# Attention scores contracted over 128 rows in four column strips instead of over 32 rows in 32x32 tiles

## The chip, the cores and the metric

The kernel runs on one core of a Trainium2 chip. The metric is the device time of one execution in microseconds (us), median over several executions. A profile is one such execution; its span runs from the first to the last instruction, so it is a little shorter than the metric. TensorE is called PE below, its weight loads PEld, VectorE DVE, ScalarE ACT, GpSimd POOL. "Granted clock" is the share of full speed that PE's clock was given. Each run has a state, fast or slow; only fast runs are compared. What is said here of the chip is read from the profiles and runs of this case, or called a reading or an estimate.

## The reference, cut to what matters

A block with a memory: 64 segments of 32 tokens, one after the other, each with 8 memory tokens that the segment before produced. 32 heads of 128 dimensions, then a feed-forward layer (FFN) with squared ReLU. Layer norms and residuals around both.

```python
for s in range(n_seg):                       # 64, a serial chain through mem
    h = jnp.concatenate([mem, xs], axis=1)   # 8 + 32 tokens, 640 wide
    q, k, v = (einsum('btd,dhe->bhte', h, W) for W in (Wq, Wk, Wv))   # 32 heads x 128
    scores = jnp.einsum('bhqe,bhke->bhqk', q, k) * scale
    p = _softmax(jnp.where(mask, scores, -1e9), axis=-1)
    o = jnp.einsum('bhte,hed->btd', jnp.einsum('bhqk,bhke->bhqe', p, v), Wo)
    mem = o[:, :M]
    outs.append(o[:, M:])
# h = x + attention; out = h + w2 . relu(w1 . norm(h) + b1)^2 + b2
```

## The kernel before

One block is four segments (`sp` = 0 to 3); a call of `step` handles one segment. The 40 keys of a segment are split: a main part of 32 (8 memory tokens and 24 of the segment's own) and a tail part with the last 8, which is kept for the four segments of a block together. The projections of q, k and v (`ps`) put four quarters of the output side by side on four strips of 32 partitions. ACT copies them to bf16 and DVE transposes them in 32x32 squares. In this kernel a strip `g` held whole heads, so after the transpose a head lay as four squares (`eb`) of 32 rows on one strip, and a score needed four matmuls that each contract over 32 rows:

```python
for g in range(G):                                   # masks: 16 matmuls
    r = slice(32 * g, 32 * g + 32)
    for c in range(G):
        nc.tensor.matmul(A(g)[32 * c:32 * c + 32, 0:AC], lhsT=id32[r, :], rhs=mask[r, sp, :], start=True, ...)
for lhsT, q1, off, n in ((kT, NQ, 0, NQ), (kt, 16, MC, 16)):   # main keys, then tail keys
    for i2 in range(2):
        for eb in range(4):
            for c in range(G):
                bl = (i2 * 4 + c) * 4 + eb
                for g in range(G):                   # 2 x 2 x 4 x 4 x 4 = 256 matmuls
                    r = slice(32 * g, 32 * g + 32)
                    nc.tensor.matmul(A(g)[32 * c:32 * c + 32, off + i2 * n:off + (i2 + 1) * n],
                                     lhsT=lhsT[r, bl, :], rhs=qT[r, bl, 0:q1], start=False, stop=(eb == 3), ...)
for t in range(2):
    nc.scalar.activation(out=p[:, 2 * t:2 * t + 2], in_=A2[t][:, :, 0:AC], func=ACT.Exp, scale=SCALE)
run(full, ...)       # a slice of FFN matmuls on PE while ACT computes Exp
# ... pz = sums over keys (2 matmuls), Ln, Exp, again a slice of FFN, pn = p * rz (2 DVE products)
# ... values: 64 matmuls of 32x128 tiles, main and tail keys alternating, then oT <- A
run(strip, ...)      # units of the next block's projections (pst) while oT is copied
wo_units(...)        # pw: 128 matmuls of 128x32 tiles, 160 columns each
run(strip, ...)      # more units while o goes to the next segment's HT
```

`full` and `strip` are lists of PE work of other blocks that fills the waits of the serial chain. `HT` is the input of a segment, transposed; a segment can't begin before the one before it has given its `o`.

The softmax here doesn't subtract the row's maximum and nothing guards it: scores larger than these inputs give would overflow.

Of the kernel before, what the change touches and what calls it, by code (L numbers as in the profile page):

```python
# [7 lines left out]
ACT = mybir.ActivationFunctionType  # L8
ALU = mybir.AluOpType
F32 = mybir.dt.float32  # L10
BF16 = mybir.dt.bfloat16
ET = mybir.EngineType

D, H, E, M, SEG, S, F = 640, 32, 128, 8, 32, 2048, 1728
G = 4
# [5 lines left out]
TL = 8  # L21
NQ = 40
# [3 lines left out]
SCALE = float(E) ** -0.5  # L26
EPS = 1e-5
NEG = -30000.0
MC = 2 * NQ
AC = MC + 32  # L30
PO = 128


@with_exitstack
def memory_transformer_kernel(ctx, tc, xa, xb, mem0, wq_d, wk_d, wv_d, wo_d, cst, wf_d, b1_d, out):
    nc = tc.nc
    pool = lambda name, bufs, **k: ctx.enter_context(tc.tile_pool(name=name, bufs=bufs, **k))
    const = pool("const", 1)
    s1, s2, s3, s4 = pool("s1", 1), pool("s2", 2), pool("s3", 3), pool("s4", 4)
    wfp = pool("wfp", WB)  # L40
    mm = pool("mm", 4, space=bass.MemoryType.PSUM)
    at = pool("at", 1, space=bass.MemoryType.PSUM)
# [4 lines left out]
    o_main = dram.tile([S // SEG, G, SEG, DG], BF16)  # L47
    o_tail = dram.tile([NB, G, SEG, DG], BF16)

    cs = const.tile([128, 128 + 128 + 32 + 4 * AC], BF16)  # L50
    ident, onesblk, id32 = cs[:, 0:128], cs[:, 128:256], cs[:, 256:288]
    mask = cs[:, 288:].rearrange("p (s a) -> p s a", s=4)
    wq, wk, wv = (const.tile([128, DC, H * E], BF16, name=n) for n in ("wq", "wk", "wv"))
    wo = const.tile([128, H, D], BF16)
    eps_t = const.tile([128, 1], F32)
# [33 lines left out]
    def flush():  # L89
        while late:  # L90
            late.pop(0)[1]()
# [14 lines left out]
    def run_side(n):  # L106
        while side and n > 0:
            side.pop(0)()
            n -= 1
# [71 lines left out]
    def blocks(row):  # L181
        return row[:].rearrange("p (b r) -> p b r", r=32)

    def half(w, lhs, n, vr=None):
        ps = mm.tile([128, 512], F32, tag="mm", name="ps")
        pass_units(w, lhs, n, ps)
        if vr is not None:
            nc.scalar.copy(out=vr[:, n * 512:(n + 1) * 512], in_=ps[:])  # L188
            return None
        row = s4.tile([128, 512], BF16, tag="row", name="row")  # L190
        nc.scalar.copy(out=row[:], in_=ps[:])  # L191
        return row
# [135 lines left out]
    def step(b, sp):  # L328
        HT, tl = HTs[b], tails[b]
        lhs = lambda c: HT[:, c * 128 + 32 * (3 - sp):c * 128 + 32 * (4 - sp)]  # L330
        qT = s1.tile([128, 32, NQ], BF16, tag="qT", name="qT")
        kT = s1.tile([128, 32, SEG], BF16, tag="kT", name="kT")
        vr = s1.tile([128, 1024], BF16, tag="vr", name="vr")
        qt = tl["q"][:].rearrange("p (b s t) -> p b s t", s=4, t=TL)
        nc.gpsimd.tensor_copy(out=qT[:, :, 0:TL], in_=qt[:, :, sp, :])
        for w, dst in ((wq, lambda n: qT[:, n * 16:(n + 1) * 16, TL:NQ]),
                       (wk, lambda n: kT[:, n * 16:(n + 1) * 16, :])):
            for n in range(2):
                row = half(w, lhs, n)
                nc.vector.transpose(out=dst(n), in_=blocks(row))  # L340
                run_side(1)
        for n in range(2):
            half(wv, lhs, n, vr)
            run_side(1)

        A2 = [at.tile([128, 2, 512], F32, tag=f"A{t}", name="A") for t in range(2)]

        def A(g):
            return A2[g // 2][:, g % 2]
        for g in range(G):  # L350
            r = slice(32 * g, 32 * g + 32)
            for c in range(G):
                nc.tensor.matmul(A(g)[32 * c:32 * c + 32, 0:AC], lhsT=id32[r, :], rhs=mask[r, sp, :], start=True,  # L353
                                 stop=False, skip_group_check=True)
        kt = tl["k"][:].rearrange("p (b r) -> p b r", r=32)
        for lhsT, q1, off, n in ((kT, NQ, 0, NQ), (kt, 16, MC, 16)):
            for i2 in range(2):
                for eb in range(4):
                    for c in range(G):
                        bl = (i2 * 4 + c) * 4 + eb  # L360
                        for g in range(G):
                            r = slice(32 * g, 32 * g + 32)
                            nc.tensor.matmul(A(g)[32 * c:32 * c + 32, off + i2 * n:off + (i2 + 1) * n],  # L363
                                             lhsT=lhsT[r, bl, :], rhs=qT[r, bl, 0:q1], start=False, stop=(eb == 3),
                                             skip_group_check=True)
        p = s1.tile([128, G, AC], BF16, tag="p", name="p")
        for t in range(2):
            nc.scalar.activation(out=p[:, 2 * t:2 * t + 2], in_=A2[t][:, :, 0:AC], func=ACT.Exp, scale=SCALE)  # L368
        share = sum(u[0] for u in full) / ((FS - sp) % 4 + 1)
        run(full, 0.84 if share > 1.9 else share / 2)  # L370
        flush()

        pz = mm.tile([128, 512], F32, tag="mm", name="pz")
        nc.tensor.matmul(pz[:, 0:320].rearrange("p (g a) -> p g a", g=G), lhsT=onesblk, rhs=p[:, :, 0:MC],  # L374
                         start=True, stop=False, skip_group_check=True)
        nc.tensor.matmul(pz[:, 0:320].rearrange("p (g i q) -> p g i q", g=G, i=2)[:, :, :, 0:16], lhsT=onesblk,  # L376
                         rhs=p[:, :, MC:AC].rearrange("p g (i q) -> p g i q", i=2), start=False, stop=True,
                         skip_group_check=True)
        nc.scalar.activation(out=pz[:, 0:320], in_=pz[:, 0:320], func=ACT.Ln)
        rz = s1.tile([128, G, MC], BF16, tag="rz", name="rz")  # L380
        nc.scalar.activation(out=rz[:].rearrange("p g a -> p (g a)"), in_=pz[:, 0:320], func=ACT.Exp, scale=-1.0)  # L381
        run(full, share - 0.84 if share > 1.9 else share / 2, True)
        if turns:
            turns.pop(0)()
        pn = s1.tile([128, G, AC], BF16, tag="pn", name="pn")
        nc.vector.tensor_tensor(out=pn[:, :, 0:MC], in0=p[:, :, 0:MC], in1=rz[:], op=ALU.mult)  # L386
        nc.vector.tensor_tensor(out=pn[:, :, MC:AC].rearrange("p g (i q) -> p g i q", i=2),
                                in0=p[:, :, MC:AC].rearrange("p g (i q) -> p g i q", i=2),
                                in1=rz[:].rearrange("p g (i q) -> p g i q", i=2)[:, :, :, 0:16], op=ALU.mult)


        for i2 in range(2):
            for g in range(G):
                j = i2 * 4 + g
                o0_ = PO + j * NQ
                for c in range(G):
                    r = slice(32 * c, 32 * c + 32)
                    nc.tensor.matmul(A(c)[:, o0_:o0_ + NQ], lhsT=vr[r, j * 128:(j + 1) * 128],  # L398
                                     rhs=pn[r, g, i2 * NQ:(i2 + 1) * NQ], start=(j == 0), stop=False,
                                     skip_group_check=True)  # L400
                for c in range(G):
                    r = slice(32 * c, 32 * c + 32)
                    nc.tensor.matmul(A(c)[:, o0_:o0_ + 16], lhsT=tl["v"][r, j * 128:(j + 1) * 128],  # L403
                                     rhs=pn[r, g, MC + i2 * 16:MC + (i2 + 1) * 16], start=False, stop=True,
                                     skip_group_check=True)
        oT = [s1.tile([128, 8, NQ], BF16, tag=f"oT{c}", name="oT") for c in range(G)]
        for c in (0, 2, 1, 3):
            dst, src = oT[c][:].rearrange("p j q -> p (j q)"), A(c)[:, PO:PO + 8 * NQ]
            if c < 2:
                nc.scalar.copy(out=dst, in_=src)  # L410
            else:
                nc.vector.tensor_copy(out=dst, in_=src)
            nc.gpsimd.tensor_copy(out=oTts[b][:, c * 8:(c + 1) * 8, sp * TL:(sp + 1) * TL], in_=oT[c][:, :, 0:TL])  # L413
        flush()
        run(strip, 0.86 if sp > 0 else 0.84)

        pw = mm.tile([128, 512], F32, tag="mm", name="pw")
        wo_units(lambda s: oT[s // 8][:, s % 8, TL:NQ], pw, slots_all)
        o = s3.tile([128, DG], BF16, tag="o", name="o")
        nc.scalar.copy(out=o[:], in_=pw[:, 0:DG])  # L420
        nc.sync.dma_start(out=o_main[b * 4 + sp].rearrange("g r d -> (g r) d"), in_=o[:])
        nb, nsp = (b, sp + 1) if sp < 3 else (b + 1, 0)
        if nb < NB:
            put_memory(nb, nsp, o)
        run(strip, 1.28 if sp < 3 else 100)
# [13 lines left out]
    for b in range(NB):  # L439
# [8 lines left out]
        for sp in range(4):  # L448
            if sp > 0 and b + 1 < NB:
                w, which = ((wq, "q"), (wk, "k"), (wv, "v"))[sp - 1]  # L450
# [76 lines left out]
```

## Time and profile before

The median before is 1514.01 us, of 6 runs. Here are lines of the page of its profile: the span, the busy time of PE and PEld, the granted clock in 40 slices (in tenths), the instruction queue (packets, MB, share) and the shares of the chain that ended last.

```profile
span 1505.5 us, 90498 instructions
PE 1193.7 (79%) x43200; PEld 863.1 (57%) x43200; DVE 470.8 (31%) x1076; ACT 454.7 (30%) x1009; POOL 164.9 (11%) x468
PEclk9888889989899898998898899888899899889987
...
q8 instruction: 337, 5.52, 1.5%
...
PE 76%; issue 15%; DMA 1%; DVE 1%; ACT 1%; POOL 0%; POOLq 0%; ACTq 0%; DVEq 0%; SPq 0%
```

PE bounds the kernel, but 15% of the chain is "issue": PE waited for nothing that the profile shows. The view of waits says where (engine, line, what it waited for, us in all, times, longest).

```profile
PE A L363 <- issue: 152.4, 76, 3.0
PE pw L218 <- issue: 49.1, 37, 3.0
...
PE pwt L218 <- issue: 15.4, 12, 1.6
PE A L398 <- DVE pn L386: 8.8, 10, 1.4
...
PE A L403 <- DVE pn L387: 1.5, 5, 0.4
```

The score matmuls (line 363) are the main place. The timeline shows one of them; columns are start, duration of the merged group, engine, line, operation, tile (rows*columns of the array and shapes), count and the idle time before.

```profile
710.55 0.87 PE L218 MATMUL pw<-wo,oT 128*32 128x160 bf16 x38 [1.62 <-issue]
...
711.20 1.52 PE L177 MATMUL pst<-wq,hTt 128*32 128x512 bf16 x24
...
712.49 2.39 PE L177 MATMUL ps<-wq,HT 128*32 128x512 bf16 x40
...
714.65 2.39 PE L177 MATMUL ps<-wk,HT 128*32 128x512 bf16 x40
...
716.81 2.39 PE L177 MATMUL ps<-wv,HT 128*32 128x512 bf16 x40
...
719.12 0.27 PE L353 MATMUL A<-cs 32*32 32x112 bf16 x16
...
719.18 1.30 PE L363 MATMUL A<-qT,kT 32*32 32x40 bf16 x128
...
720.30 0.65 PE L363 MATMUL A<-qT,kt 32*32 32x16 bf16 x58
...
723.08 0.69 PE L363 MATMUL A<-qT,kt 32*32 32x16 bf16 x70 [2.12 <-issue]
...
723.70 0.99 PE L310 MATMUL psy<-wf,f1T 128*128 128x320 bf16 x6
```

Count the matmuls from the one gap to the next: 38 + 24 + 40 + 40 + 40 + 16 + 128 + 58 = 384. Each has a weight load, so 768 instructions, which is exactly three times 256. This holds over the trace: of 115 stretches over 1 us in which neither PE nor PEld was busy, 104 lie at a multiple of 256 PE instructions from one another. The instruction queue moved 5.52 MB in 337 packets, each of 16,384 bytes. That is 64 bytes an instruction if a packet holds 256 of them. So this text reads the gaps as waits for the next block of instructions (256 of them; where this text speaks of blocks that are fetched, arrive or begin, it means these, and not the kernel's blocks of four segments). While it has them, PE runs the 512 score instructions of a segment, two blocks, in about 2.1 us. That is faster than blocks arrive: of the 135 that begin at such a multiple of 256 after a gap over 0.3 us, the median began 3.56 us after the block before, and where two in a row did so (28 times), the second began 3.45 to 4.03 us after the first.

The clock hangs on this too. Its records hold only full rate and half rate (67 stretches of each); at a mean of 0.889, half rate took (1 - 0.889) x 2 x 1505.5 = 334 us. Of its 67 stretches at half rate, 57 begin within 2 us of the end of a gap over 1 us in the scores; moments taken at random would give about 12.

### The profile page before, as it was taken

What the parts mean: (1) busy time and instruction counts of PE and PEld (TensorE: products, weight loads), DVE (VectorE), ACT (ScalarE), POOL (GpSimd) and SP (SyncE); (2) the same over time, 40 slices, a digit from 0 to 9 for tenths busy, and PEclk for the clock granted to TensorE, in tenths of its full rate; (3) what the DMA queues carried; (4) which work ended last, traced back from release to release, by engine and by line L of the source; (5) the groups of instructions that cost most, each with busy time, mean ns of one, the idle gap of its engine ahead of it and who ended that gap; (6) DMA issues with size and microseconds to landing.
All of it is one profiled execution on the core that took longest, in us unless ns stands there. A gap on an engine that the chain in (4) does not pass through costs nothing.

```text
span 1505.5 us, 90498 instructions
## 1 busy us (share of the span) xinstructions
PE 1193.7 (79%) x43200; PEld 863.1 (57%) x43200; DVE 470.8 (31%) x1076; ACT 454.7 (30%) x1009; POOL 164.9 (11%) x468
## 2 busy tenths in 40 slices
PE   0777887888888787888878888788888878788875
PEld 0454556565566666656656656566555555655553
DVE  0322233333332333333333323233233233333322
ACT  0333332333333232332333333232333223233220
POOL 0000011010111101001010101101011110101111
PEclk9888889989899898998898899888899899889987
DMA  9500012122122212212222212212212212221235
GB/s 399 225 5 10 16 32 73 53 78 75 46 67 72 67 59 72 71 45 77 63 63 72 71 42 71 81 48 79 70 49 66 71 54 71 67 75 44 71 93 172
DMA packets 63441, 114.18 MB, mean 76 GB/s; under 512 B 25696, under 2 KB 31968, under 8 KB 60640
## 3 DMA queue, kind: packets, MB, share of 16 engines
q1 hardware_dynamic: 61344, 96.15, 20.7%
q10 hardware_dynamic: 1728, 12.25, 2.0%
q8 instruction: 337, 5.52, 1.5%
q14 instruction: 32, 0.26, 0.1%
HBM read 102.47 MB, written 5.90 MB: 72 GB/s over the span
## 4 chain that ended last, share of the span: by engine, by line
PE 76%; issue 15%; DMA 1%; DVE 1%; ACT 1%; POOL 0%; POOLq 0%; ACTq 0%; DVEq 0%; SPq 0%
PE ps L177 27%; PE pw L218 10%; PE A L363 10%; PE pst L177 8%; PE psf L278 7%; PE psy L310 6%; PE pwt L218 3%; PE A L398 2%; PE pz L374 1%; DMA wf<-in_wf_dram 1%; PE A L403 1%; PE pt L140 1%; PE A L353 1%; PE pz L376 0%; DVE pn L386 0%
## 5 line engine op out<-in xcount | busy, mean ns | idle before, releaser
L177 PEld LDWEIGHTS <-HT 128*32 128x32 bf16 x7680 | 248.4, 97 | 170.0 <-issue 5.1
L218 PE MATMUL pw<-wo,oT 128*32 128x160 bf16 x8192 | 172.0, 241 | 51.7 <-issue 49.1
L363 PE MATMUL A<-qT,kt 32*32 32x16 bf16 x8192 | 86.4, 179 | 145.4 <-issue 145.4
L218 PEld LDWEIGHTS <-oT 128*32 128x32 bf16 x8192 | 156.7, 101 | 72.0 <-issue 58.8
L191 ACT CAST row<-ps 128x512 bf16<-128x512 f32 x256 | 148.0, 584 | 116.3 <-PE ps L177 115.5
L363 PEld LDWEIGHTS <-kt 32*32 32x32 bf16 x8192 | 74.6, 89 | 151.4 <-issue 151.2
L177 PE MATMUL ps<-wq,HT 128*32 128x512 bf16 x2560 | 154.5, 380 | 4.0 <-DVE HT L171 2.3
L177 PE MATMUL ps<-wk,HT 128*32 128x512 bf16 x2560 | 153.4, 379 | 0.0
L177 PE MATMUL ps<-wv,HT 128*32 128x512 bf16 x2560 | 153.3, 379 | 0.0
L291 DVE TENSOR_SCALAR r<-psf,b1f 128x128 bf16<-128x128 f32 x224 | 67.4, 345 | 214.2 <-PE psf L278 211.3
L340 DVE STREAM_TRANSPOSE qT<-row 128x512 bf16<-128x512 bf16 x128 | 91.1, 712 | 124.6 <-ACT row L191 124.6
L368 ACT ACTIVATE p<-A 128x224 bf16<-128x224 f32 x128 | 39.0, 355 | 275.6 <-PE A L363 275.6
L278 PE MATMUL psf<-hnT,wf 128*128 128x128 bf16 x1120 | 115.3, 286 | 6.1 <-issue 4.5
L294 POOL TENSOR_TENSOR f1T<-r 128x256 bf16<-128x256 bf16 x96 | 59.9, 627 | 526.6 <-DVE r L291 490.8
L310 PE MATMUL psy<-wf,f1T 128*128 128x320 bf16 x448 | 111.9, 414 | 5.2 <-DMA wf<-in_wf_dram 3.3
L413 POOL COPY oTt<-oT 128x64 bf16<-128x64 bf16 x256 | 49.1, 238 | 575.0 <-ACT oT L410 575.0
L278 PEld LDWEIGHTS <-wf 128*128 128x128 bf16 x1120 | 103.0, 134 | 11.5 <-issue 6.6
L340 DVE STREAM_TRANSPOSE kT<-row 128x512 bf16<-128x512 bf16 x128 | 91.0, 711 | 57.4 <-ACT row L191 57.4
L386 DVE TENSOR_TENSOR pn<-p,rz 128x320 bf16<-128x320 bf16 x64 | 20.6, 321 | 243.3 <-ACT rz L381 243.2
L363 PE MATMUL A<-qT,kT 32*32 32x40 bf16 x8192 | 84.9, 185 | 9.4 <-issue 7.0
L188 ACT CAST vr<-ps 128x512 bf16<-128x512 f32 x128 | 75.0, 587 | 49.3 <-PE ps L177 49.3
L420 ACT CAST o<-pw 128x160 bf16<-128x160 f32 x64 | 18.7, 293 | 226.5 <-PE pw L218 226.5
(55 smaller groups left out, 1154.1 us busy)
## 6 DMA issues: line engine op xcount, KB each, us to landing
wf<-in_wf_dram SPq DMA_DIRECT2D x224, 320.0 KB
wq<-in_wq_dram ACTq DMA_DIRECT2D x3, 1024.0 KB
wk<-in_wk_dram ACTq DMA_DIRECT2D x3, 1024.0 KB
wv<-in_wv_dram ACTq DMA_DIRECT2D x3, 1024.0 KB
xt<-in_xa_dram SPq DMA_DIRECT2D x16, 160.0 KB
wo<-in_wo_dram SPq DMA_DIRECT2D x2, 1280.0 KB
wo<-in_wo_dram ACTq DMA_DIRECT2D x2, 1280.0 KB
o_main<-o SPq DMA_DIRECT2D x64, 40.0 KB
```

The lines of the kernel that those rows point to most:

```text
L177: nc.tensor.matmul(ps[32 * g:32 * g + 32, :], lhsT=lhs(c), rhs=w[:, c, g * EG + n * 512:g * EG + (n + 1) * 512], start=(c == 0), stop=(c = ...
L188: nc.scalar.copy(out=vr[:, n * 512:(n + 1) * 512], in_=ps[:])
L191: nc.scalar.copy(out=row[:], in_=ps[:])
L218: nc.tensor.matmul(ps[32 * g:32 * g + 32, 0:DG], lhsT=lhs(s), rhs=wo[:, s, g * DG:(g + 1) * DG], start=(s == slots_all[0]), stop=(s == slo ...
L278: nc.tensor.matmul(ps[:, u * 128:(u + 1) * 128], lhsT=wfv[:, u, c], rhs=h["hnT"][:, c, :], start=(c == 0), stop=(c == DC - 1), skip_group_ ...
L291: nc.vector.tensor_scalar(out=r[0:fs, u, :], in0=ps[0:fs, u * 128:(u + 1) * 128], scalar1=b1f[0:fs, fc:fc + 1], scalar2=0.0, op0=ALU.add, ...
L294: nc.gpsimd.tensor_tensor(out=f1T[:, 2 * k:2 * k + 2, :], in0=r[:], in1=r[:], op=ALU.mult)
L310: nc.tensor.matmul(h["ps"][:, 0:320], lhsT=f1T[:, fc + i, :], rhs=wf[:, (m % 4) * 320:(m % 4 + 1) * 320], start=(fc + i == 0), stop=(fc + ...
L340: nc.vector.transpose(out=dst(n), in_=blocks(row))
L363: nc.tensor.matmul(A(g)[32 * c:32 * c + 32, off + i2 * n:off + (i2 + 1) * n], lhsT=lhsT[r, bl, :], rhs=qT[r, bl, 0:q1], start=False, stop= ...
L368: nc.scalar.activation(out=p[:, 2 * t:2 * t + 2], in_=A2[t][:, :, 0:AC], func=ACT.Exp, scale=SCALE)
L413: nc.gpsimd.tensor_copy(out=oTts[b][:, c * 8:(c + 1) * 8, sp * TL:(sp + 1) * TL], in_=oT[c][:, :, 0:TL])
```

## The change: its intent and the diff

The weights of q and k are reordered on the host so that a strip holds a quarter of *every* head. After the same transposes the 128 partitions of one square column then hold one whole head, and a score is one matmul that contracts over 128 rows. Four of them lie side by side in four column strips. That makes 64 score matmuls a segment in place of 256, and 8 mask matmuls in place of 16. All scores of a segment (448 columns) fit one PSUM tile of 512 columns, which now comes from the rotating pool `mm` of four; the values keep the other pool. Exp becomes one instruction. Projections, softmax sums, values and pw keep their sizes.

```diff
-        A2 = [at.tile([128, 2, 512], F32, tag=f"A{t}", name="A") for t in range(2)]
-        for g in range(G):
-            r = slice(32 * g, 32 * g + 32)
-            for c in range(G):
-                nc.tensor.matmul(A(g)[32 * c:32 * c + 32, 0:AC], lhsT=id32[r, :], rhs=mask[r, sp, :], start=True, ...)
+        A = mm.tile([128, 512], F32, tag="mm", name="A")
+        for c in range(G):
+            r = slice(32 * c, 32 * c + 32)
+            nc.tensor.matmul(A[r, 0:MC].rearrange("p (i q) -> p i q", i=8)[:, :, 16:NQ], lhsT=id32, rhs=mask, ...)
+        for c in range(G):
+            r = slice(32 * c, 32 * c + 32)
+            nc.tensor.matmul(A[r, MC:AC], lhsT=id32, rhs=tmask[:, sp, :], start=False, stop=False, ...)
-        for lhsT, q1, off, n in ((kT, NQ, 0, NQ), (kt, 16, MC, 16)):
-            for i2 in range(2):
-                for eb in range(4):
-                    for c in range(G):
-                        bl = (i2 * 4 + c) * 4 + eb
-                        for g in range(G):
-                            r = slice(32 * g, 32 * g + 32)
-                            nc.tensor.matmul(A(g)[32 * c:32 * c + 32, off + i2 * n:off + (i2 + 1) * n],
-                                             lhsT=lhsT[r, bl, :], rhs=qT[r, bl, 0:q1], start=False, stop=(eb == 3), ...)
+        for lhsT, n, off in ((kT, NQ, 0), (kt, 16, MC)):
+            for i in range(8):
+                for c in range(G):
+                    nc.tensor.matmul(A[32 * c:32 * c + 32, off + i * n:off + (i + 1) * n], lhsT=lhsT[:, i * 4 + c, :],
+                                     rhs=qT[:, i * 4 + c, 0:n], start=False, stop=True, ...)
-        for t in range(2):
-            nc.scalar.activation(out=p[:, 2 * t:2 * t + 2], in_=A2[t][:, :, 0:AC], func=ACT.Exp, scale=SCALE)
+        nc.scalar.activation(out=p[:], in_=A[:, 0:AC], func=ACT.Exp, scale=SCALE)
...      # softmax sums, products pn and values: the same work, indexed by head differently
...      # host: weights of q and k by quarters of heads, of v and o by heads, masks to match
```

## The prediction

> **What bounds it now.** PE. The chain of waits is 76% PE and 15% "issue"; DVE and ACT are busy 31% and 30% (page, part 1). One step (64 of them) takes 22.1 us, start of mask to start of mask, in the trace in order of time. Three things inside it are not arithmetic:

> 1. *Starved issue.* The waits view has 152.4 us of "issue" before the score matmuls, 49.1 before pw, 15.4 before pwt. Counting PE's instructions (weight loads and matmuls) in the trace, nearly every gap falls at a multiple of 256 instructions with a constant offset, and the instruction queue moved 337 packets of 16 KB (part 3), one per 256. [...] in starved stretches blocks begin 3.45 to 3.75 us apart. A step's 512 score instructions run in about 1.9 us when present (about 4.2 ns each), so PE starves about 2.3 us there.
> 2. *Score length.* Mask and scores together, gap included: 4.98 us mean per step, 319 us in all.
> 3. *Half clock.* The granted clock is 0.889; its records hold 335 us at half rate, typically 3.4 or 6.8 us beginning at the score gap. [...] windows whose matmuls streamed under about 0.38 of the array's columns were followed by half rate. It falls on the FFN slices: score to pz takes 0.76 us warm and 1.50 cold, pz to the value matmuls 1.40 and 2.07. Means are 1.26 and 2.01: 1.1 us a step lost.

> **What changes, per step.** 256 score matmuls become 64, 16 masks become 8: 400 fewer PE instructions of about 1350 (25,600 in all, 100 blocks). The mask's tiles are 32x32 and the scores' 128x32, one more switch of tiling. Cost of a new pair, estimated between the 32x32 pair (9 ns) and the pw pair in the same 128x32 tiling (18 ns at 160 columns): about 16 ns, so 1.0 us, plus masks 0.25 and the last matmul's 0.18 latency: about 1.4 us against 4.98. The 144 instructions fit beside slower work, so the score gap should nearly vanish. Exp becomes one of 448 columns for two of 224: about 0.54 us (estimate from 429 ns at 320 and 586 at 512) for 0.61, hidden behind FFN. Ln, Exp, pn, values, oT, pw keep their sizes. A moves to the rotating PSUM pool; its predecessors are evacuated early, so I expect little waiting.

> **On the path.** All of it: 3.55 us x 64 = 227 us. With gaps gone, clock windows stay above 0.38: about 70 us more. pw's fetch gaps stay, shifted: about 1 us a step. Replaying the trace with the block rule gives about 1150; this sum about 1205 plus, for the unprofiled metric, a few us. I take 1190: about 17.2 us a step.

> **Right if:** PE instructions about 60,800; instruction packets about 237; issue waits before scores under 20 us (from 152), before pw and pwt 40 to 90; score span 1.2 to 1.7 us; granted clock at least 0.96; score to pz near 0.76; waits for pn grow but stay under 30 us.

> **Wrong if:** weight loads to column strips sharing all rows serialize[...]; fetch gaps reappear in pw or the projections; clock still drops; A's buffer makes FFN wait; weight DMAs arrive late at the faster pace.

> Predicted 1190 us, eight in ten within 1140 to 1245. Faster by over 2%: 0.98; within 2%: 0.01; slower: 0.01.

The span of 1505.5 us less 227 and about 70 is about 1208, which it gives as about 1205. The "block rule" of the replay is an estimate: it spaces blocks by the 3.45 us read from starved stretches of the trace of before. The "windows" are the steps in which the clock records of before change: 66 of their 67 stretches at half rate last a multiple of 3.41 us.

## The result, and the profile after

The changed kernel took 1179.14 us (median of 10 runs) against 1512.58 us (20 runs), a ratio of 0.7786 with a 95% interval of 0.7764 to 0.7809. A ratio here is the mean time of one kernel's fast runs over that of the other's of the same rounds, so not quite the ratio of the medians quoted. Executions over 1.5% slower than the fastest of the same kernel are left out of the means. The result is correct. The same lines of the page:

```profile
span 1177.4 us, 64836 instructions
PE 989.7 (84%) x30400; PEld 722.4 (61%) x30400; DVE 477.1 (41%) x1076; ACT 449.9 (38%) x945; POOL 164.8 (14%) x468
PEclk9988999999999999999999999999999999999987
...
q8 instruction: 237, 3.88, 1.3%
...
PE 76%; issue 8%; DMA 6%; DVE 5%; ACT 3%; POOL 1%; SPq 1%; ACTq 0%; DVEq 0%; POOLq 0%
```

Exactly 100 packets of instructions are gone, "issue" fell from 15% to 8% of a shorter chain, and the clock row is at 9 from the first segments on (mean 0.973, half rate for (1 - 0.973) x 2 x 1177.4 = 64 us). The waits (line 358 is the scores, 390 the values, 217 pw and pwt):

```profile
PE pw L217 <- issue: 67.9, 44, 3.5
...
PE O L390 <- DVE pn L380: 20.6, 50, 1.4
PE O L390 <- DVE pn L381: 9.8, 28, 0.4
PE pwt L217 <- issue: 8.1, 8, 1.3
```

No issue wait before the scores is left. What stayed is the one before pw, somewhat larger (67.9 us from 49.1), and the values now wait for the product pn, 30.4 us in all from 10.3. The timeline of one segment's scores (PE alone):

```profile
712.77 0.31 PE L348 MATMUL A<-cs 128*32 128x192 bf16 x4
712.85 0.22 PE L352 MATMUL A<-cs 128*32 128x128 bf16 x1
712.91 0.18 PE L358 MATMUL A<-qT,kT 128*32 128x40 bf16 x1
712.91 0.23 PE L352 MATMUL A<-cs 128*32 128x128 bf16 x3
712.94 0.43 PE L358 MATMUL A<-qT,kT 128*32 128x40 bf16 x31
713.18 0.44 PE L358 MATMUL A<-qT,kt 128*32 128x16 bf16 x32
713.55 1.01 PE L277 MATMUL psf<-hnT,wf 128*128 128x128 bf16 x15
```

The whole stretch from the first mask to the FFN's first matmul is 0.78 us, where it was 4.58 us (719.12 to 723.70) in the segment shown of before. Within a run of score matmuls, starts lie 8 ns apart in the median in *both* kernels: a 128x32 matmul with its weight load costs hardly more than a 32x32 one (8.2 ns against 7.5, the mean of the starts less than 40 ns apart), and there are a quarter as many.

Means over the 64 segments, from the matmuls' times in the two traces, show where the time came from. The last column is the difference times 64.

| stretch of a segment | before, us | after, us | saved, us |
|---|---|---|---|
| first mask to end of scores | 4.98 | 0.90 | 261 |
| end of scores to pz (FFN slice, Exp) | 1.26 | 0.76 | 32 |
| end of pz to values (FFN slice, Ln, Exp, pn) | 2.01 | 1.45 | 36 |
| values | 0.72 | 0.93 | -13 |

They add up to 316 us of the 328 us between the two spans. The second and third rows are the clock: before, these stretches take 0.77 and 1.40 us in the median at full rate and 1.50 and 2.07 us at half rate; after, nearly all run at full rate and take 0.76 and 1.40 us. The fourth row is new waiting, within the values, for the second product pn. The rest of a segment nearly cancels: pw with its wait grew from 3.46 to 3.74 us, while pz itself (0.55 to 0.36 us) and what lies around pw shrank.

### The profile page after: what moved, and what is told of

Same layout as the page of the kernel before. It is cut to its first block, busy times and chain, and to the rows that moved or that the text cites. A ratio compares the mean times of both kernels' runs of the same rounds, so it can differ in the third digit from the quotient of the medians.

```text
span 1177.4 us, 64836 instructions
## 1 busy us (share of the span) xinstructions
PE 989.7 (84%) x30400; PEld 722.4 (61%) x30400; DVE 477.1 (41%) x1076; ACT 449.9 (38%) x945; POOL 164.8 (14%) x468
## 4 chain that ended last, share of the span: by engine, by line
PE 76%; issue 8%; DMA 6%; DVE 5%; ACT 3%; POOL 1%; SPq 1%; ACTq 0%; DVEq 0%; POOLq 0%
PE ps L176 35%; PE pw L217 14%; PE pst L176 9%; PE psy L309 4%; PE O L390 4%; PE pwt L217 4%; PE A L358 3%; PE psf L277 2%; DMA wo<-in_wo_dram 2%; DMA wk<-in_wk_dram 2%; DVE r L290 1%; ACT rz L375 1%; DVE pn L381 1%; DVE pn L380 1%; ACT pz L373 1%
## 5 line engine op out<-in xcount | busy, mean ns | idle before, releaser
L176 PEld LDWEIGHTS <-HT 128*32 128x32 bf16 x7680 | 254.3, 98 | 170.4 <-issue 12.9
L217 PE MATMUL pw<-wo,oT 128*32 128x160 bf16 x8192 | 171.5, 240 | 70.3 <-issue 67.9
L176 PE MATMUL ps<-wq,HT 128*32 128x512 bf16 x2560 | 159.1, 387 | 4.9 <-issue 2.6
L170 DVE STREAM_TRANSPOSE HT<-o 128x160 bf16<-128x160 bf16 x64 | 22.1, 345 | 206.8 <-ACT o L407 206.8
L397 ACT CAST oT<-O 128x320 bf16<-128x320 f32 x128 | 48.2, 429 | 97.3 <-PE O L390 97.3
L309 PE MATMUL psy<-wf,f1T 128*128 128x320 bf16 x448 | 74.6, 308 | 6.7 <-DMA wf<-in_wf_dram 6.6
L399 DVE CAST oT<-O 128x320 bf16<-128x320 f32 x128 | 56.9, 486 | 52.6 <-PE O L390 52.6
L176 PEld LDWEIGHTS <-hTt 128*32 128x32 bf16 x1920 | 51.8, 99 | 41.6 <-issue 12.3
L277 PE MATMUL psf<-hnT,wf 128*128 128x128 bf16 x1120 | 74.5, 222 | 0.9 <-DVE hnT L263 0.6
L277 PEld LDWEIGHTS <-wf 128*128 128x128 bf16 x1120 | 65.6, 99 | 3.1 <-issue 0.7
L390 PE MATMUL O<-pn,vr 32*128 32x40 bf16 x2048 | 47.2, 179 | 21.1 <-DVE pn L380 20.6
```

What stands on the lines that cost most here:

```text
L176: nc.tensor.matmul(ps[32 * g:32 * g + 32, :], lhsT=lhs(c), rhs=w[:, c, g * EG + n * 512:g * EG + (n + 1) * 512], start=(c == 0), stop=(c = ...
L217: nc.tensor.matmul(ps[32 * g:32 * g + 32, 0:DG], lhsT=lhs(s), rhs=wo[:, s, g * DG:(g + 1) * DG], start=(s == slots_all[0]), stop=(s == slo ...
L277: nc.tensor.matmul(ps[:, u * 128:(u + 1) * 128], lhsT=wfv[:, u, c], rhs=h["hnT"][:, c, :], start=(c == 0), stop=(c == DC - 1), skip_group_ ...
L309: nc.tensor.matmul(h["ps"][:, 0:320], lhsT=f1T[:, fc + i, :], rhs=wf[:, (m % 4) * 320:(m % 4 + 1) * 320], start=(fc + i == 0), stop=(fc + ...
L390: nc.tensor.matmul(O[c][:, i * NQ:i * NQ + n], lhsT=lhsT[r, i * 128:(i + 1) * 128], rhs=pn[r, off + i * n:off + (i + 1) * n], start=(i == ...
L399: nc.vector.tensor_copy(out=dst, in_=src)
```

## The experiments

Theory A: what the change removed is instructions, and PE starved for them. Rivals: B, the array work of the removed matmuls; C and D, about the clock; E, something in the old tiling, masks or buffers. Later runs add their own (F to I), named in what was expected of them.

### The number of instructions put back, in the new tiling

```diff
-                    nc.tensor.matmul(A[...], lhsT=lhsT[:, i * 4 + c, :], rhs=qT[:, i * 4 + c, 0:n], stop=True, ...)
+                    for rep in range(4):         # and scale=SCALE / 4 in Exp, so the result stays right
+                        nc.tensor.matmul(A[...], lhsT=lhsT[:, i * 4 + c, :], rhs=qT[:, i * 4 + c, 0:n], stop=(rep == 3), ...)
```

> The changed kernel, each score matmul issued four times on the same operands (the sum is four times too large and the scale of the exponential is a quarter, so the result stays right): 256 score matmuls of 128x32 tiles a step, as many PE instructions as before apart from the masks. Theory A (PE starves for instructions: a block of 256 can't begin sooner than about 3.45 us after the last): the gap in the scores is back, score span 4 us or more, issue waits before the score matmuls over 100 us, granted clock back to about 0.89, 1460 to 1550 us. Theory B (the gain is the array work of the removed matmuls): 192 more pairs at the measured 7.5 ns is 1.4 us a step, so about 1270 us, no gap.

It took 1488.25 us (4 runs), 0.9842 of before [0.9784, 0.9899]; correct. Its waits:

```profile
PE A L359 <- issue: 131.5, 68, 2.7
PE pw L217 <- issue: 77.1, 45, 3.4
```

The gap in the scores is back, and the segment's mask and scores take 4.83 us. At about 8 ns a pair, 192 more pairs account for about 98 us (192 x 8 ns x 64); the kernel lost some 310. Theory B is out as the whole explanation; the time of the pairs themselves is about a third of it. One expectation missed: the clock was 0.941 in the profile (0.923 to 0.941 in the four runs), not 0.89. A later pair of runs takes that up.

With two issues each instead of four:

> The changed kernel, each score matmul issued twice (scale halved, result right): 128 score matmuls a step, 128 PE instructions more. Theory A: replaying the trace with the block rule gives about 84 us more, so 1240 to 1290 us, as starved gaps appear in some of the steps or grow before pw. Theory B (array work only): 64 pairs at 7.5 ns are 0.5 us a step, about 1210 us.

This took 1240.85 us, 0.8203 [0.8158, 0.8247], 62 us more than the change. Scores grew by 0.60 us a segment to 1.50 (39 us in all, little more than the 0.52 us of 64 pairs at 8.1 ns), and the issue wait before them is only 2.0 us; the wait before pw grew from 67.9 to 83.3 us:

```profile
PE pw L217 <- issue: 83.3, 47, 3.1
```

So the first 64 extra pairs cost 62 us and the next 128 cost 247, almost twice as much a pair: that is the shape theory A would give, in which waiting sets in only when the burst is long enough (before the scores 2.0 us of it at 128 pairs, 131.5 us at 256). The replay had said 84, so it overstated starving for this size.

### The old tiling with the new number of instructions

```diff
-                for eb in range(4):
+                for eb in range(1):              # a quarter of the contraction: wrong on purpose
```

(made to the kernel before, with `stop=True`)

> The kernel before, with a quarter of its score matmuls (a quarter of the contraction; the result is wrong on purpose): 64 matmuls of 32x32 tiles a step, as many as after the change, in the old tiling, with the old masks and PSUM. Theory A (number of instructions is what counts, not the rows that they contract): within about 20 us of the changed kernel, 1165 to 1205 us, clock about 0.97. Theory E (32x32 tiles, their masks or the old buffers cost something of their own): clearly slower than the changed kernel, over 1220 us.

It took 1188.76 us, 0.7869 [0.7828, 0.791]; the result is wrong, as intended. Its page and waits:

```profile
PE 999.6 (84%) x30912; PEld 722.5 (61%) x30912; DVE 477.2 (40%) x1076; ACT 454.4 (38%) x1009; POOL 165.2 (14%) x468
...
q8 instruction: 241, 3.95, 1.3%
```

```profile
PE pw L218 <- issue: 70.6, 40, 3.5
```

This is the strongest result. Old tiles, old masks, old PSUM layout, two Exp instructions, and still within 10 us of the changed kernel, with the clock at 0.971 and no issue wait before the scores. The 128 rows matter because they let one instruction do what four did, not because wide contraction is faster in itself. What is left for theory E is about 10 us, and it is not in the old masks, scores or Exp: from the first mask to the end of the scores this run takes 0.81 us a segment against 0.90 of the changed kernel, and from there to pz 0.77 against 0.76. Its span is 8.6 us longer because it reaches the first mask 2.6 us later and spends about 0.15 us more a segment in pw and from pw to the next mask; why was not tested.

### What idle time alone does to the clock

```diff
         nc.scalar.activation(out=p[:], in_=A[:, 0:AC], func=ACT.Exp, scale=SCALE)
+        dl = s1.tile([128, 320], BF16, tag="dl", name="dl")
+        nc.scalar.copy(out=dl[:], in_=p[:, 0:320])
+        for _ in range(3):
+            nc.scalar.copy(out=dl[:], in_=dl[:])
+        nc.tensor.matmul(A[:, 511:512], lhsT=onesblk, rhs=dl[:, 319:320], start=False, stop=True, ...)
```

> The changed kernel, with a chain of four copies on ACT after the exponential and one one-column matmul that waits for it ahead of the FFN slice: PE stands idle about 2.4 us after the scores of each step, with no instructions added but one pair. It tells what idle time alone does to the clock. Theory C (idle in a 3.4 us window is what halves the clock, whatever causes the idle): the granted clock falls to about 0.9, score to pz beyond the gap and pz to the values slow down by some 1 us a step, so the cost is the idle of about 150 us plus about 65: 1360 to 1420 us. Theory D (the low clock before came from the 32x32 matmuls themselves): the clock stays near 0.97 and the cost is the idle alone, about 1330 us.

It took 1358.5 us, 0.9017 [0.8946, 0.9089]. The idle time and the clock:

```profile
PE A L366 <- ACT dl L365: 169.5, 64, 2.6
...
PE pw L217 <- issue: 45.6, 37, 3.0
```

```profile
core 0: 1341.9 us, clock 0.941
```

Idle alone, with one pair on PE and four copies on ACT more a segment, takes the clock from 0.973 to 0.941 (fast runs: 0.964 to 0.977 for the changed kernel, 0.930 to 0.941 here), so D falls as the whole story. But C was too strong: half rate took (1 - 0.941) x 2 x 1341.9 = 158 us, about half of the 334 of before, though the idle is a little longer than there (2.65 us a segment for 2.4). The profile also shows a repayment: the wait before pw fell from 67.9 to 45.6 us. Blocks that arrive while PE stands idle would explain it; that was not shown.

### Do the rows at work count for the clock?

The four-fold kernel and the idle one both end at 0.941 with a gap like that of before. What before had and they lack is 32 rows at work instead of 128. First the four-fold kernel again, then the same with a quarter of the rows:

```diff
-                        lhsT=lhsT[:, i * 4 + c, :], rhs=qT[:, i * 4 + c, 0:n]
+                        lhsT=lhsT[0:32, i * 4 + c, :], rhs=qT[0:32, i * 4 + c, 0:n]     # wrong on purpose
```

> The kernel that issues each score matmul four times, again, as the yardstick of the next one on the same chip: about 0.984 of the time of before, granted clock 0.94 with some 180 us at half rate.

> The same, but each of its 256 score matmuls reads the first 32 rows only (32x32 tiles in one row group; the result is wrong on purpose). Same number of instructions, same columns streamed; a quarter of the rows at work. The yardstick has as wide a gap in the scores as before, yet about half of the time at half rate (176 us for 335). Theory H (the clock gate counts how many rows are at work, so the small tiles of before are part of why its clock fell): the time at half rate rises towards 300 us, the clock to 0.90 or lower, 10 to 30 us slower than the yardstick. Theory I (rows don't count; another difference, such as the old masks, makes the rest): clock and time as the yardstick, within 5 us.

The yardstick took 1489.98 us (0.9845 of before [0.9814, 0.9877]), the one with 32 rows 1503.48 us (0.9948 [0.9921, 0.9976]). The summary of the core for each, yardstick first:

```profile
core 0: 1498.3 us, clock 0.932
```

```profile
core 0: 1501.8 us, clock 0.883
```

And the wait before the scores, yardstick first:

```profile
PE A L359 <- issue: 133.9, 69, 2.9
```

```profile
PE A L359 <- issue: 132.0, 66, 2.8
```

### Smaller theories: the PSUM pool, and the new waits

A back in the pool of the values (the changed kernel again first, as the yardstick of these runs):

```diff
-        A = mm.tile([128, 512], F32, tag="mm", name="A")
+        A = at.tile([128, 2, 512], F32, tag="O0", name="A")[:, 0]
```

> The changed kernel again, on the chip of the three that follow, as their yardstick: 1170 to 1190 us.

> The changed kernel with the scores' PSUM tile A back in the pool of the attention results (it shares two banks with O), so that the rotating pool of four serves only the projections and the FFN. Theory F (A in the rotating pool makes matmuls wait for evacuations): 10 us or more faster, fewer waits of PE. Theory G (A's predecessors are evacuated in time, as the prediction had it): within 5 us of the changed kernel.

1178.19 us (0.7787 [0.7758, 0.7815]) and 1178.57 us (0.7783 [0.7752, 0.7814]). The pool makes no difference that these runs can see.

The values of the main keys first, then those of the tail keys:

```diff
-        for i in range(8):
-            for lhsT, n, off in ((vr, NQ, 0), (tl["v"], 16, MC)):
+        for lhsT, n, off in ((vr, NQ, 0), (tl["v"], 16, MC)):
+            for i in range(8):
```

> The changed kernel with the 32 value matmuls of the main keys before the 32 of the tail keys, not alternating by head. After the change the value matmuls wait twice, for the first and for the second product pn (20.6 and 9.8 us in the waits view), and their span is 0.93 us mean against 0.68 in the stalled steps of before. If the second wait is on the path, the main matmuls cover it: wait for the second pn under 2 us, span of the values near 0.75 us, 8 to 15 us faster. If the fetch of instructions before pw binds, the gap before pw grows by what was saved and the time stays within 3 us.

1171.38 us, 0.7749 [0.7722, 0.7776]. Its waits:

```profile
PE pw L217 <- issue: 74.5, 43, 3.8
...
PE O L390 <- DVE pn L380: 20.8, 50, 1.4
...
PE O L390 <- DVE pn L381: 4.9, 28, 0.2
```

The values shrink from 0.93 to 0.77 us a segment (10 us in all) and the second wait halves, though it does not fall under 2 us as expected. The median is 7 us lower; the two intervals overlap, so that is a lean. The wait before pw, 67.9 us in the changed kernel's profile, is 74.5 us here, so that part of what was saved may have come back there.

On top of that, one unit of projection moved ahead of the values:

```diff
+        else:                                  # no transposes in this step
+            run(strip, 0.1)                    # and 0.22 us less behind pw
         pn = s1.tile([128, AC], BF16, tag="pn", name="pn")
```

> The previous one, and one unit of the next block's projections (10 PE instructions, 0.216 us) moved from behind pw to just before the value matmuls, in the steps without transposes there. It fills the wait for the first pn (20.6 us). If that wait is on the path: another 5 to 12 us faster, the wait for pn under 10 us. If what is behind pw then no longer covers the way from o to the next HT, the waits for HT grow by as much (0.2 us a step) and nothing is won.

1169.39 us for the median of all six runs. One run at 1152.43 us makes three of the others count as slow, so the ratio of 0.7682 rests on three runs and is not used. The wait for the first pn fell to 10.9 us, nearly as expected. In time this run is inconclusive. The same in every step, with the reordered kernel again as its yardstick:

> The kernel with the main keys' value matmuls before the tail keys', again, as the yardstick of the next one: about 0.775 of the time of before.

> As the kernel that moved one unit of the next block's projections ahead of the value matmuls, but in every step, also in those with transposes there. The wait for the first pn falls from 20.8 us to under 7 us. If that is on the path: 8 to 14 us faster than the yardstick. If the gap before pw grows as the earlier waits shrink (it went from 67.9 to 74.5 and 76.0 us in the last two steps), under 5 us.

The yardstick took 1174.75 us (0.7772 [0.7743, 0.78]), only 3 us below the changed kernel, so the lean of the reordering got weaker; this kernel took 1168.05 us (0.7735 [0.7707, 0.7763]). Its waits:

```profile
PE pw L217 <- issue: 70.2, 42, 3.5
...
PE O L391 <- DVE pn L381: 7.6, 10, 1.1
```

The wait for the first pn went from 21.0 to 7.6 us, and the median is 6.7 us lower, between what the two theories said. Against the changed kernel, 0.7735 stands to 0.7787: with both edits some 0.7% or 10 us. It beats the kernel before clearly; against the changed one (up to 0.7763 here, from 0.7758 there) and against its yardstick the intervals still touch, so this is a lean too, the strongest of them. The wait before pw, the largest left, was not removed by anything tried here.

## Why the prediction was right or wrong

The range held the result: 1179.14 us for 1190 predicted, 1140 to 1245.

**Starved issue: right, and shown.** Score instructions outran the blocks, and removing 25,600 PE instructions (scores and masks) removed the wait before the scores. The counts came out as predicted, 60,800 PE instructions and 237 packets. Two experiments bear it out from both sides: the old number of instructions in the new tiling (1488 us) and the new number in the old tiling (1189 us). In the trace of before, a block that PE was starving for began 2.28 to 2.68 us (middle 80%, median 2.38) after its packet started, and the packet itself took about 0.98 us. The prediction's "3.45 us apart" is the sum of that and the time from one block's start to the next packet's, about 1.1 us.

**Score length: right in direction, mis-sized.** The prediction put masks and scores at "about 1.4 us against 4.98" and 227 us; they take 0.90 us and saved 261. The term that was wrong is "about 16 ns" for a new pair: it measures about 8 ns. It was interpolated towards pw's 18 ns, but pw streams 160 columns and these 40 or 16. The feared serializing of weight loads to strips that share all rows did not come: the starts of the new pairs lie 8 ns apart, where one of their weight loads is recorded as 93 ns long (median). A small step was wrong outright: "the mask's tiles are 32x32 ... one more switch of tiling". The identity now spans all 128 partitions (zeros below the first 32 rows), so the masks run in 128x32 tiles, as the timeline shows, and there is no switch.

**Half clock: right in size, too simple in its rule.** The two FFN stretches saved 32 + 36 = 68 us for "about 70 us more" and the clock is 0.973 for "at least 0.96". But "under about 0.38 of the array's columns" described one trace. It sorts 329 of the 330 full-rate windows of before, and no such threshold sorts the four-fold kernel's 369 without 20 misses among 42 drops. The runs showed that idle time counts (0.973 to 0.941) and rows at work count (0.932 to 0.883). What exactly halves the clock stays open. The low stretches of before are multiples of 3.41 us, all but the last, in which the run ends.

**The gap before pw: right.** "40 to 90" us; 67.9 + 8.1 = 76.0.

**The wait for pn: just missed.** "Under 30 us"; it is 20.6 + 9.8 = 30.4, and the second part also stretched the values by 0.2 us a segment. The first part was foreseen: at full clock the FFN slices no longer cover Ln, Exp and the product.

**A in the rotating pool: right.** No effect found.

The sum of the parts in the prediction, 1205, erred by the pair's cost; the replay, 1150, erred the other way. The figure between them came out well partly by luck: these two errors oppose.

## What to carry to other kernels

When the gaps of PE bear the name "issue", count instructions between them. Here 104 of 115 gaps over 1 us lay at multiples of 256, the mark of PE eating instructions faster than they arrived; then the cheapest matmul was the one that needed not be issued, so a layout that contracts over all 128 rows was worth more than small tiles that lie side by side (1179 us for 1513, and 1189 with the old tiles at the new number). Look at bursts, not at the mean: of 1,350 instructions a segment, PE starved most where some 500 came within about 2 us. And a gap cost twice here, once by itself (152.4 us before the scores) and once by the half clock around it (68 us of the FFN slices), though what a later starving stretch gives back must be set against that: the wait before pw was 22 us shorter with the idle time put in.
